# Sink attention feeding a sticky mixture of experts on one core: moving the split of the second head group, the order of GpSimd's group work, and the PSUM banks of the routing

## The chip, the core and the metric

The kernel runs on one core of one Trainium2 chip. The core has a matrix engine (PE, with its weight loads shown apart as PEld), a vector engine (DVE), a scalar engine (ACT), GpSimd (POOL) and a sync engine (SP) that issues most of the DMAs. Each engine works through its own list of instructions in order and waits on semaphores of the others. The metric is the device time of one execution in microseconds (us), lower is better; "before" and "after" are medians of several runs. An execution taken by the profiler gives the trace, with a span (first to last instruction of the program) a little shorter than its device time.

## The reference

For 4 batches, 8 heads, 768 positions and a head width of 64 the program computes attention in which a query sees the first 4 positions (sinks) and the last 128 (the window), and feeds its output to a mixture of 8 experts in which a token may stay with the expert of the token before it:

```python
keep = is_sink | in_window
scores = np.where(keep, scale * np.matmul(q, k.transpose(0, 1, 3, 2)), -1000000000.0)
a = np.exp(scores - np.max(scores, axis=-1, keepdims=True))
x = np.matmul(a / (np.sum(a, axis=-1, keepdims=True) + 1e-09), v)    # then (B, S, H * D)

logits = np.einsum('bsd,de->bse', x, w_gate)
local_gate = 1.0 / (1.0 + np.exp(-np.einsum('bsd,de->bse', x, w_local).squeeze(-1)))
for b in range(B):
    prev_e = -1
    for s in range(S):
        fresh_e = int(np.argmax(logits[b, s]))
        if s == 0 or local_gate[b, s] < 0.5: e = fresh_e
        else: e = prev_e if prev_e >= 0 else fresh_e
        prev_e = e
        p = softmax(logits[b, s])
        out[b, s] = p[e] * (np.maximum(x[b, s] @ w1[e], 0.0) @ w2[e])
```

All inputs and outputs are float32. (`softmax` stands here for three lines of the reference.)

## The kernel before

**Two halves.** Up to about 239 us of the span the kernel runs the attention with the routing of tokens to experts; after that it runs the experts one after another. The change touches the first half only, in the path for a narrow window (`attention(True)`; the other path is not run on these inputs).

**Groups and blocks.** The attention is cut into 8 groups of four heads (two groups for a batch), counted from 0 here: group g is batch g // 2. A group has 6 blocks of 128 queries, so there are 48 blocks, n = 0 to 47, and block n belongs to group n // 6. Within a block the four heads are two pairs, c = 0 and c = 1. The heart of the schedule is one loop over n that works on four blocks at once: it scores block n on PE (`score`, L635), subtracts the maximum on DVE (`out`, L647) and takes the exponential on ACT (L650), transposes the weights of block n - 1 on PE (`turn`, L665) and copies them back on ACT (`turned`, L672), turns and splits the sink part of n - 1 (L655, L676, L682, L686), multiplies block n - 2 with the values (`apply`, L696 and L701), and brings block n - 3 back into row order with its gate logits (`collect` L587, `back` L591, `finish` L607 and L611). PE, DVE and ACT run in exactly the order in which the loop is written (a manual schedule). POOL and SP are ordered by the framework's scheduler, except where `tc.issue_after` or an explicit dependency says otherwise.

**Splits.** The scores are products of float32 values, done as three products of a high and a low part. So the queries and keys of every group have to be split before its first block: a cast to the high part (`copy`, L135) and a subtraction for the low part (`low`, L140), for two pairs, keys (800 columns) and queries (768 columns). The result goes into `hq` (odd groups) or `w_a` (even groups). Group 0 is split piece by piece on DVE, ACT and POOL; all others were split on POOL alone, eight instructions for a group. `qk_split` makes four steps for a group, numbered 0: keys of pair 0, 1: queries of pair 0, 2: keys of pair 1, 3: queries of pair 1, and the table `HEADS` says at which unit (k = 2 i + c for block i of the running group) which steps of the next group are issued. An entry of `behind` becomes an explicit wait of the next cast on another instruction ("a port of its own"): in group 0 on the latest low part that POOL was given (`lows["gpsimd"]`), in later groups on DVE's L647 of the running block. Each group has a further small split on POOL, the sink rows of its values (`sinks`, L579 and L580).

**Loads.** SP issues, in an order chained by `queue`, the raw queries and keys (four buffers, so the load of a pair waits until the split of the pair four earlier has read its buffer), the values and the sink rows.

**Routing.** When the second group of a batch is done, a generator (`routing`) works through the batch's tokens in small steps that the tables `SCORED` (after the scores of a block) and `CLOSED` (at the end of a block) interleave with the blocks: gate logits and their maximum on DVE (L276 to L294), two transposes with a scan (L310, L314, L319), one-hot rows (L329, L331), positions (L358, L361), normalisation and slot numbers on DVE (L335 to L371), and six indirect DMAs that POOL issues to scatter the rows by expert (L376). For batch 0 these steps fall in blocks 14 to 23, for batch 1 in 26 to 35, for batch 2 in 38 to 45 by a table of its own; the last batch is handled after block 47. `early_rows` follows for batch 2: a count of the first expert's rows (L413, L414, L416 to L422), two loads of such rows by SP, three small DVE operations (L434 to L436), a broadcast over PE (`shown`, L439, L440) and two DVE operations on its result (L443).

**PSUM.** The transposes of the weights use a pool `ps_t` of two banks in turn; the sink turn and `back` share one bank in `ps_b`. The routing's results used that same single bank.

```python
ps_t = pool("ps_t", 2 if fast else 1, space=PS)
ps_b = pool("ps_b", 1, space=PS)
if fast:
    ps_m, m_tag = ps_b, "b"
```

Of the kernel before, what the change touches and what calls it, by code (L numbers as in the profile page):

```python
# [47 lines left out]
FILL = 5  # L48
FIRST_P = 4
SCORED = {5: 1, 6: 1, 9: 1, 10: 1}, {41: 1, 42: 1, 43: 1, 44: 1, 45: 1, 47: 1}  # L50
CLOSED = {2: 1, 3: 1, 4: 1, 5: 1, 6: 1, 9: 1, 10: 1, 11: 1}, {38: 1, 39: 2, 41: 1, 42: 1, 43: 1, 44: 2, 45: 2, 46: 1, 47: 1}
LOADS = {0: (2,), 2: (3,), 3: (0,), 4: (1,), 6: (4,), 8: (5,)}
HEADS = {4: (0, 1), 5: (2, 3)}, {2: (0, 1), 3: (2, 3)}, {0: (0, 1), 1: (2, 3)}
FIRST = 0, 2, 4, 6, 1, 3, 5, 7
NPR = HG // 2
SENG = ("vector", "gpsimd", "act", "vector"), ("act", "gpsimd", "act", "vector")
LENG = SENG[0], ("act", "gpsimd", "act", "gpsimd")
REST = (("vector", "gpsimd", "act", "gpsimd"),) * NPR
ENGS = (("gpsimd", "gpsimd", "gpsimd", "gpsimd"),) * NPR
RAW = 7200  # L60
RAW_W = RAW + 56
NZ = 4
# [12 lines left out]
def kernel(ctx, tc, qkd, vn, vs, w1, w2, nw, c_misc, c_ident, c_idw, c_small,  # L75
# [61 lines left out]
    lows, behind, opened = {}, [], []  # L137
# [402 lines left out]
    def attention(fast):  # L540
# [3 lines left out]
        with ExitStack() as st:  # L544
            def pool(nm, bufs, **kw):
                return st.enter_context(tc.tile_pool(name=nm + sfx, bufs=bufs, **kw))
# [3 lines left out]
            ps_t = pool("ps_t", 2 if fast else 1, space=PS)  # L550
            ps_a = pool("ps_a", 1, space=PS)
            ps_b = pool("ps_b", 1, space=PS)
            ps_s = pool("ps_s", 2, space=PS)
            if fast:
                ps_m, m_tag = ps_b, "b"
                pe_p = pool("pep", 2)
            else:
                ps_m, m_tag = pool("ps_m", 1, space=PS), "m"
                p1 = pool("p1", 1)
                relg = p1.tile([P, 2, S], F32, name="relg")  # L560
                nc.sync.dma_start(relg, c_all)
# [210 lines left out]
            if fast:  # L772
                ng = len(groups)
                preps = [{"heads": []} for _ in groups]
                preps[0]["heads"] = heads0
                gst = [group_steps(b, g, preps[gi]) for gi, (b, g) in enumerate(groups)]

                def head(gi, h):
                    if h == 0:
                        preps[gi]["steps"], preps[gi]["heads"] = qk_split(gi, ENGS)  # L780
                    preps[gi]["steps"][h]()

                def slot(u, gi, k):
                    nx = gi + 1
                    if gi == 0:
                        for x in LOADS.get(k, ()):
                            qk_load(x) if x > 1 else gst[nx]["load"][x]()
                        if k == RK:
                            gst[0]["sinks"]()
                    if nx >= ng:  # L790
                        return
                    for h in HEADS[gi and 2 - gi % 2].get(k, ()):
                        if gi and not h:
                            behind.append(u["dve"])
                        elif not gi:
                            behind.append(lows["gpsimd"])
                        with tc.issue_after(opened[-1].ins) if gi % 2 and h else ExitStack():
                            head(nx, h)
                        if nx == ng - 1 and h >= 1:
                            free.append(True)  # L800
                    if gi and k in (4, 5):
                        gst[nx]["load"][k - 4]()
                    if k == 2 * NBLK - 1:
                        gst[nx]["sinks"]()
                    if gi:
                        last.clear()

# [36 lines left out]
                for n in range(nb):  # L844
# [49 lines left out]
                    weights(n, now[0] if now else None)  # L894
                    steps(CLOSED, n)
                while pend:
# [3 lines left out]
                b, g = B - 1, G - 1  # L900
# [127 lines left out]
    with branch.Else():  # L1028
        attention(False)
# [299 lines left out]
    for c in range(2):  # L1329
        h, l = [t[:, c, :] for t in w1_of(1)]  # L1330
# [158 lines left out]
```

## Time and profile before

| | |
|---|---|
| median of 3 runs | 569.78 us (569.46 to 572.39) |
| profiled execution | 566.28 us, span 564.5 us |
| mean granted TensorE clock | 0.969 |
| PE busy | 525.7 us (93%) |
| DVE busy | 332.6 us (59%) |
| ACT busy | 282.8 us (50%) |
| POOL busy | 230.6 us (41%) |
| DMA | 80.55 MB, mean 143 GB/s |

Rows of the trace read: start and duration in us, engine (PE, PEld, DVE, ACT, POOL, SP; a "q" behind it is its sequencer), line of the kernel, operation, tile written <- tiles read with shapes, and the number of like instructions merged into the row. A bracket at the end gives how long the engine was idle before the row and what ended that. Rows that sum up a stretch of time give, for each engine, its busy time and in brackets its instructions, then the granted clock (1.00 is full speed) and the DMAs' share. Rows that group instructions by their form end with the total busy time, the mean of one in ns, and the idle time before them.

### The profile page before, as it was taken

To read this page: it belongs to the slowest core of one execution; us is meant where nothing else is said; L and a number is where in the kernel's file an instruction comes from. 1 tells how busy PE (TensorE), PEld (TensorE's weight loads), DVE (VectorE), ACT (ScalarE), POOL (GpSimd) and SP (SyncE) were. 2 spreads that over 40 slices of the span, in tenths; PEclk is the share of its full clock that TensorE was granted. 3 is DMA by queue.
4 is the path that set the end of the run, shared out by engine and by line. 5 is a ranking of instruction groups with operands and counts; after the bars stand their busy time and mean duration, and the time that the engine had idled before them with its cause. 6 is when DMAs were issued, how large, how long until landed. Compare 5 with 4: busy or idle time off the path is not lost. (4 is left out here: it accounts for less than half of the span.)

```text
span 564.5 us, 11848 instructions
## 1 busy us (share of the span) xinstructions
PE 525.7 (93%) x3935; PEld 449.0 (80%) x3935; DVE 332.6 (59%) x1260; ACT 282.8 (50%) x861; POOL 230.6 (41%) x196
## 2 busy tenths in 40 slices
PE   6979999889989988999999999999999899999994
PEld 3768878677877867878888888979878598889893
DVE  5647887777768867744348193735456737353321
ACT  4848888577847867253344271706324344124120
POOL 3658706760874073237350262535304434104101
PEclk8779999999979998999999999999999989999998
DMA  8354332550435035167491383848215484111000
GB/s 292 142 212 151 134 100 72 193 177 36 153 138 206 2 114 188 58 208 233 116 352 35 124 274 121 311 109 304 99 50 199 168 272 148 56 44 37 20 24 36
DMA packets 31020, 80.55 MB, mean 143 GB/s; under 512 B 3678, under 2 KB 6366, under 8 KB 30816
## 3 DMA queue, kind: packets, MB, share of 16 engines
q1 hardware_dynamic: 26064, 65.41, 34.2%
q0 software_dynamic: 4176, 12.64, 6.0%
q14 instruction: 149, 1.22, 0.7%
q8 instruction: 55, 0.90, 0.6%
q10 hardware_dynamic: 576, 0.39, 0.2%
HBM read 63.41 MB, written 16.06 MB: 141 GB/s over the span
## 5 line engine op out<-in xcount | busy, mean ns | idle before, releaser
L650 ACT ACTIVATE pef<-smf,biasf 128x264 f32<-128x264 f32 (+2 forms) x192 | 93.6, 489 | 41.5 <-DVE biasf L647 41.4
L1175 ACT ACTIVATE hq<-h 128x32 fp32r<-128x32 f32 (+4 forms) x112 | 32.1, 317 | 142.1 <-PE h L1164 92.0
L647 DVE CUSTOM_DVE_ANT_0 smf<-sf,mask 128x264 f32<-128x264 f32 (+2 forms) x192 | 66.7, 403 | 17.5 <-PE sf L635 6.4
L1140 DVE SCALAR_TENSOR_TENSOR hq<-h,hq 128x32 fp32r<-128x32 f32 (+4 forms) x112 | 34.4, 332 | 66.4 <-ACT hq L1175 66.0
L1213 PE MATMUL late<-w_a,hq 128*128 128x512 f32 (+2 forms) x288 | 69.0, 394 | 0.0
L1213 PEld LDWEIGHTS late<-w_a,hq 128*128 128x128 f32 (+2 forms) x288 | 50.8, 179 | 13.0 <-issue 0.2
L1195 POOL DMA_INDIRECT out_dram<-ot_d,oi_d x18 | 19.4, 1077 | 94.2 <-DVE ot_d L1194 74.7
L665 PE MATMUL tpf<-ident,pef 128*128 128x128 f32 x352 | 54.9, 297 | 1.9 <-ACT ptf L672 1.1
L701 PE MATMUL avf<-ptf,v 128*64 128x128 f32 x704 | 52.4, 288 | 2.7 <-issue 2.7
L672 ACT COPY ptf<-tpf 128x512 f32<-128x512 f32 (+1 forms) x96 | 51.1, 532 | 6.9 <-remote 3.4
L665 PEld LDWEIGHTS tpf<-ident,pef 128*128 128x128 f32 x352 | 40.6, 149 | 9.9 <-ACT ptf L672 3.6
L701 PEld LDWEIGHTS avf<-ptf,v 128*64 128x64 f32 x704 | 39.6, 141 | 8.3 <-issue 3.4
L1213 PE MATMUL late<-w_b,hq 128*128 128x512 f32 (+1 forms) x168 | 39.9, 393 | 0.0
L607 DVE TENSOR_TENSOR xb<-bkf,rsf 128x256 f32<-128x256 f32 x48 | 20.3, 423 | 27.7 <-ACT ptsf L682 24.9
L650 ACT ACTIVATION_READ_ACCUMULATOR pef<-smf,biasf 128x1 f32 x192 | 36.4, 189 | 0.0
L591 PE MATMUL bkf<-idw,xtf 128*128 128x146 f32 x192 | 34.5, 305 | 1.9 <-DVE xtf L587 1.5
L1213 PEld LDWEIGHTS late<-w_b,hq 128*128 128x128 f32 (+1 forms) x168 | 30.6, 184 | 7.0
L1164 PEld LDWEIGHTS h<-x_a,w_c 128*128 128x128 f32 x288 | 34.8, 192 | 1.4 <-issue 1.1
L1164 PE MATMUL h<-x_a,w_c 128*128 128x256 f32 x288 | 35.4, 284 | 0.4 <-DMA out_dram<-ot_d,oi_d 0.4
L1070 POOL TENSOR_TENSOR w_c<-raw,w_c 128x1024 fp32r<-128x1024 f32 x10 | 25.2, 2521 | 24.6 <-ACT w_c L1069 21.7
L376 POOL DMA_INDIRECT xs<-xb,slotf x24 | 23.4, 974 | 26.1 <-DVE xb L371 18.2
L1070 POOL TENSOR_TENSOR w_a<-raw,w_a 128x1024 fp32r<-128x1024 f32 x10 | 24.6, 2460 | 22.8 <-ACT w_a L1069 18.0
(228 smaller groups left out, 1081.4 us busy)
## 6 DMA issues: line engine op xcount, KB each, us to landing
raw<-in_dram SPq DMA_DIRECT2D x53, 512.0 KB
raw<-in_dram SPq DMA_DIRECT2D x14, 800.0 KB
v<-in_dram SPq DMA_DIRECT2D x7, 768.0 KB
xr_0n<-xs SPq DMA_DIRECT2D x18, 258.0 KB
raw_w<-in_dram SPq DMA_DIRECT2D x7, 512.0 KB
raw<-in_dram SPq DMA_DIRECT2D x10, 256.0 KB
xs<-zrow SPq DMA_DIRECT2D x9, 258.0 KB
xr_0r<-xs SPq DMA_DIRECT2D x8, 258.0 KB
```

Source lines behind the costliest of these rows:

```text
L376: s_i = nc.gpsimd.indirect_dma_start(out=xs[:, :], out_offset=bass.IndirectOffsetOnAxis(ap=slot[:, j:j + 1].bitcast(U32), axis=0), in_=xb[ ...
L591: mm = nc.tensor.matmul(bk[:, pr * WX:(pr + 1) * WX], blk["xt"][:, pr, :], idw[:, g * NPR + pr, :], start=True, stop=True, skip_group_chec ...
L647: u["dve"] = nc.vector.tensor_tensor_reduce(out=sm[:, :w], in0=sps[:, t, :w], in1=mk, scale=-0.125, scalar=BIG, op0=ALU.add, op1=ALU.min, ...
L650: nc.scalar.activation(pe[:, h, :w], sm[:, :w], AF.Exp, bias=bias[:, t:t + 1], scale=-1.0, accum_out=z[:, h, 0:1])
L665: nc.tensor.transpose(tp[:, t, k, :], pe[:, 2 * c + t, o:o + P], ident)
L672: nc.scalar.copy(pt[:, :, 0:nt, :], tp[:, :, 0:nt, :])
L701: nc.tensor.matmul(avt[ROWS[t], pr, :], prep["v"][:, j, 2 * pr + t, :], x["pt"][:, t, k, :], start=i < 2 and pr == 0 and k == 0, stop=pr = ...
L1070: todo += [lambda s=s: lo(out=l[:, s], in0=raw[:, s], in1=h.bitcast(F32)[:, s], op=ALU.subtract) for s in ([slice(0, FF)] if eng[1] == "po ...
L1140: nc.vector.scalar_tensor_tensor(out=d[:, :, 1, :], in0=h, scalar=0.0, in1=d.bitcast(F32)[:, :, 0, :], op0=ALU.max, op1=ALU.subtract)
L1164: nc.tensor.matmul(hs, w[:, k, fs], x, start=t == 0, stop=t == len(mm) - 1)
L1175: relu = nc.scalar.activation(d[:, :, 0, :], h, AF.Relu)
L1213: nc.tensor.matmul(o, a, w, start=t == 0, stop=t == len(mm) - 1, skip_group_check=half)
```

## The change: where the splits, the sink rows and the routing's banks go

There are six edits.

1. For group 1 alone (the second group, split during group 0) the cast of the queries moves from POOL to ACT; their low part stays on POOL (`ENGS` becomes two tables).
2. The steps of that split get other places (`HEADS[0]`): keys of pair 0 and of pair 1 after block 2, queries of pair 0 after block 3, queries of pair 1 after block 4. The explicit wait on the latest POOL low part goes with each step, so it now stands on ACT's casts too.
3. The sink rows of group 1 are issued behind the latest low part on POOL (`tc.issue_after`).
4. The steps after the first of a group's split are issued behind its first cast in all later groups; before, only in those split during an odd group.
5. The routing takes its PSUM tiles from the two banks of the transposes.
6. The table for the end of the attention has no routing step at the end of block 45 (two before) and three at the end of block 46 (one before). The steps moved are the loads of early rows and L434 to L436.

```diff
-CLOSED = {2: 1, 3: 1, 4: 1, 5: 1, 6: 1, 9: 1, 10: 1, 11: 1}, {38: 1, 39: 2, 41: 1, 42: 1, 43: 1, 44: 2, 45: 2, 46: 1, 47: 1}
+CLOSED = {2: 1, 3: 1, 4: 1, 5: 1, 6: 1, 9: 1, 10: 1, 11: 1}, {38: 1, 39: 2, 41: 1, 42: 1, 43: 1, 44: 2, 46: 3, 47: 1}
 LOADS = {0: (2,), 2: (3,), 3: (0,), 4: (1,), 6: (4,), 8: (5,)}
-HEADS = {4: (0, 1), 5: (2, 3)}, {2: (0, 1), 3: (2, 3)}, {0: (0, 1), 1: (2, 3)}
+HEADS = {4: (0,), 5: (2,), 6: (1,), 8: (3,)}, {2: (0, 1), 3: (2, 3)}, {0: (0, 1), 1: (2, 3)}
...
-ENGS = (("gpsimd", "gpsimd", "gpsimd", "gpsimd"),) * NPR
+ENGS = (("gpsimd", "gpsimd", "act", "gpsimd"),) * NPR, (("gpsimd", "gpsimd", "gpsimd", "gpsimd"),) * NPR
...
             if fast:
-                ps_m, m_tag = ps_b, "b"
+                ps_m, m_tag = ps_t, "t"
...
                     if h == 0:
-                        preps[gi]["steps"], preps[gi]["heads"] = qk_split(gi, ENGS)
+                        preps[gi]["steps"], preps[gi]["heads"] = qk_split(gi, ENGS[gi > 1])
...
-                        with tc.issue_after(opened[-1].ins) if gi % 2 and h else ExitStack():
+                        with tc.issue_after(opened[-1].ins) if gi and h else ExitStack():
                             head(nx, h)
...
                     if k == 2 * NBLK - 1:
-                        gst[nx]["sinks"]()
+                        with ExitStack() if gi else tc.issue_after(lows["gpsimd"].ins):
+                            gst[nx]["sinks"]()
```

In the rows that follow, the bracket names the queues whose semaphores an instruction waits for (DMAHW: a load; Pool, DVE, PE, Activation: that engine).

POOL's list in group 0, from the last low parts of group 0 (`w_a`) over the split of group 1 (`hq`) to the sink rows of group 1 (`srf_1`). Before:

```order
L140 TENSOR_TENSOR w_a<-raw,w_a 128x272 [waits DMAHW6_49,Activation_49]
L579 CAST srf_1_572<-sxf_1_350 96x256 [waits DMAHW2_49]
L580 TENSOR_TENSOR srf_1_572<-sxf_1_350,srf_1_572 32x256 [waits Pool_49]
L140 TENSOR_TENSOR w_a<-raw,w_a 128x272 [waits DVE_49,Pool_49]
L140 TENSOR_TENSOR w_a<-raw,w_a 128x272 [waits DMAHW3_49,DVE_49]
L140 TENSOR_TENSOR w_a<-raw,w_a 128x240 [waits Activation_49] x2
L135 CAST hq<-raw 128x800 [waits DMAHW6_49,Pool_49]
L140 TENSOR_TENSOR hq<-raw,hq 128x800 [waits Pool_49]
L135 CAST hq<-raw 128x768 [waits Pool_49]
L140 TENSOR_TENSOR hq<-raw,hq 128x768 [waits Pool_49]
L135 CAST hq<-raw 128x800 [waits DMAHW7_49,Pool_49]
L140 TENSOR_TENSOR hq<-raw,hq 128x800 [waits Pool_49]
```

and in the changed kernel, from the last low parts of group 0 on:

```order
L140 TENSOR_TENSOR w_a<-raw,w_a 128x240 [waits Activation_49] x2
L135 CAST hq<-raw 128x800 [waits DMAHW6_49,Pool_49]
L140 TENSOR_TENSOR hq<-raw,hq 128x800 [waits Pool_49]
L135 CAST hq<-raw 128x800 [waits DMAHW7_49,Pool_49]
L140 TENSOR_TENSOR hq<-raw,hq 128x800 [waits Pool_49]
L488 COPY xb_144<-small 128x6
L489 MEMSET xb_144 128x6x2
L261 CAST identb<-ident 128x128
L262 CAST identb<-small 128x128
L140 TENSOR_TENSOR hq<-raw,hq 128x768 [waits Activation_49] x2
L579 CAST srf_1_572<-sxf_1_350 96x256 [waits DMAHW2_49]
L580 TENSOR_TENSOR srf_1_572<-sxf_1_350,srf_1_572 32x256 [waits Pool_49]
```

The sink rows stood ahead of group 0's last low parts and now stand behind the whole split; the two casts of the queries are gone from POOL, and the low parts of the queries wait for ACT and stand last.

ACT's list in the changed kernel, from the end of block 3 (copy of its second transposes) to the start of block 5:

```order
L672 COPY ptf_0_2_1_418<-tpf_0_2_1_399 128x512 [waits Activation_49]
L135 CAST hq<-raw 128x768 [waits DMAHW6_49,Pool_49]
L650 ACTIVATE pef_0_4_0_439,sum_z<-smf_0_4_0_0_460,biasf_0_4_0_440 128x264 [waits DVE_49,Activation_49]
L650 ACTIVATE pef_0_4_0_439,sum_z<-smf_0_4_0_1_463,biasf_0_4_0_440 128x264 [waits DVE_49]
L672 COPY ptf_0_3_0_480<-tpf_0_3_0_466 128x512 [waits PE_49]
L682 CAST ptsf_482<-bkf_476 96x128 [waits PE_49]
L650 ACTIVATE pef_0_4_0_439,sum_z<-smf_0_4_1_0_484,biasf_0_4_1_448 128x264 [waits DVE_49]
L650 ACTIVATE pef_0_4_0_439,sum_z<-smf_0_4_1_1_487,biasf_0_4_1_448 128x264 [waits DVE_49]
L672 COPY ptf_0_3_1_490<-tpf_0_3_1_471 128x512 [waits Activation_49]
L135 CAST hq<-raw 128x768 [waits DMAHW7_49,Pool_49]
```

Before, the two `L135` rows are not there. Each waits for a load (DMAHW) and for POOL: by the explicit wait, the first for the low part of the keys of pair 1, the second for the low part of the queries of pair 0.

POOL's list around the first scatter (`L376`, end of group 3), with the split of group 5 (`hq`) and its sink rows (`srf_1`):

```order
-L135 CAST hq<-raw 128x768 x2
-L135 CAST hq<-raw 128x800
 L376 DMA xs<-xb_144,slotf_0_1812 25600x516 x6
 L135 CAST hq<-raw 128x800
-L140 TENSOR_TENSOR hq<-raw,hq 128x768
+L135 CAST hq<-raw 128x768
+L135 CAST hq<-raw 128x800
+L135 CAST hq<-raw 128x768
 L579 CAST srf_1_2323<-sxf_1_2093 96x256
-L140 TENSOR_TENSOR hq<-raw,hq 128x768
-L140 TENSOR_TENSOR hq<-raw,hq 128x800
 L488 COPY xb_144<-small 128x6
```

Three of the four casts stood ahead of the scatter and now stand behind it, and all four low parts stand behind the sink rows' cast, where one stood ahead of it. The same holds at the second scatter. The orders of PE and DVE are unchanged but for L434 to L436, which stand one block later. On SP the load of group 2's sink rows moves behind four loads of raw queries and keys, and the loads of the raw pairs 4 to 7 are chained 4, 6, 5, 7 instead of 6, 7, 4, 5.

## The prediction

> **What bounds the kernel now.** I read the page's part 1, then PE's idle time block by block in the timeline, because PE is busy for nearly the whole span.
>
> ```profile
> PE 525.7 (93%) x3935; PEld 449.0 (80%) x3935; DVE 332.6 (59%) x1260; ACT 282.8 (50%) x861; POOL 230.6 (41%) x196
> ```
>
> PE sets the end, and the change can win or lose only where PE stands still or its clock is halved during the attention. Three such places are touched. Other engines matter where PE waits for them. The first is the start of group 1 (block 6, from 31.08):
>
> ```profile
> 21.31 2.81 POOL L140 TENSOR_TENSOR w_a<-raw,w_a 128x272 fp32r<-128x272 f32 x4
> ...
> 24.19 0.85 POOL L135 CAST hq<-raw 128x800 fp32r<-128x800 f32 x1
> ...
> 27.08 0.82 POOL L135 CAST hq<-raw 128x768 fp32r<-128x768 f32 x1
> ...
> 33.63 0.44 PE L635 MATMUL sf<-hq 64*128 64x128 f32 x4 [2.00 <-POOL hq L135]
> ...
> 35.51 0.47 PE L635 MATMUL sf<-hq 64*128 64x128 f32 x2 [1.44 <-POOL hq L140]
> ...
> 41.17 0.97 PE L635 MATMUL sf<-hq 64*128 64x256 f32 x12
> ```
>
> PE waits 3.44 us for POOL's split and block 7 starts at 41.17, 10.1 us after block 6. The windows of 3.41 us in which the clock changes (PE, PEld, DVE, ACT, POOL busy; clock):
>
> ```profile
> 30.82:34.23 3.41, 1.24 (x16) 0.79 (x12) 2.02 (x10) 2.31 (x9) 3.27 (x3) 1.00 0.66 238
> 34.23:37.65 3.42, 2.14 (x10) 2.03 (x11) 0.58 (x5) 0.59 (x1) 1.87 (x5) 0.50 0.30 65
> 37.65:41.06 3.41, 3.41 (x25) 3.11 (x23) 0.99 (x4) 1.51 (x6) 0.00 (x0) 0.50 1.01 412
> ...
> 102.49:105.90 3.41, 1.79 (x21) 1.45 (x19) 3.28 (x11) 0.41 (x1) 2.44 (x4) 1.00 0.48 192
> 105.90:109.32 3.42, 3.34 (x39) 2.83 (x39) 2.63 (x14) 2.71 (x11) 2.81 (x3) 1.00 0.35 134
> ...
> 157.09:160.51 3.42, 1.76 (x18) 1.53 (x20) 3.34 (x15) 1.08 (x5) 2.54 (x4) 1.00 0.09 35
> 160.51:163.92 3.41, 3.41 (x28) 2.96 (x25) 1.62 (x6) 2.13 (x8) 2.50 (x4) 0.50 0.55 206
> ```
>
> The stall is paid twice: a window with 1.24 us of PE work is followed by half clock. So is one with 1.76; one with 1.79 is not.
>
> The second place is block 23, and likewise block 35, at the scatter:
>
> ```profile
> 102.86 2.39 POOL L135 CAST hq<-raw 128x768 fp32r<-128x768 f32 x3 [1.69 <-issue]
> ...
> 103.06 0.69 DVE L338 TENSOR_TENSOR exf<-exf,smf 128x48 f32<-128x48 f32 x1
> ...
> 103.67 0.84 DVE L367 TENSOR_TENSOR slf<-rksf,ohs 128x48 f32<-128x48 f32 x1
> ...
> 104.44 0.87 DVE L368 TENSOR_TENSOR exf<-exf,ohs 128x48 f32<-128x48 f32 x1
> ...
> 105.85 1.15 POOL L376 DMA_INDIRECT xs<-xb,slotf  x1 [0.59 <-DVE pkf L655]
> ...
> 105.86 0.28 PE L676 MATMUL bkf<-ident,pkf 128*96 128x128 f32 x1 [1.62 <-DVE pkf L655]
> ...
> 114.53 0.29 DVE L647 CUSTOM_DVE_ANT_0 smf<-sf,mask 128x128 f32<-128x128 f32 x1 [2.40 <-remote]
> ...
> 158.67 0.29 PE L676 MATMUL bkf<-ident,pkf 128*96 128x128 f32 x1 [1.62 <-DVE pkf L655]
> ...
> 167.33 0.29 DVE L647 CUSTOM_DVE_ANT_0 smf<-sf,mask 128x128 f32<-128x128 f32 x1 [2.42 <-PE bkf L591]
> ...
> 201.38 0.21 DVE L338 TENSOR_TENSOR exf<-exf,smf 128x48 f32<-128x48 f32 x1
> ```
>
> With a POOL cast running, L338 takes 0.69 instead of the 0.21 it takes in block 45, and each of the three ends with one of POOL's casts. PE waits 1.62 for what is queued behind them on DVE. The later long wait of DVE ends 8.68 us after the first scatter starts, with clock 1.00, and 8.7 after it in block 36, with clock 0.50; so I tie it to the scatter and expect it to stay.
>
> The third is the bank of the routing:
>
> ```profile
> 79.36 1.09 PE L665 MATMUL tpf<-ident,pef 128*128 128x128 f32 x8
> ...
> 79.47 0.79 ACT L314 COPY kff<-tff 8x768 bf16<-8x768 bf16 x1 [0.19 <-PE tff L310]
> ...
> 88.70 0.77 PE L591 MATMUL bkf<-idw,xtf 128*128 128x146 f32 x4 [0.74 <-DVE xtf L587]
> ...
> 214.25 0.35 PE L439 MATMUL shown<-early_f,one_row 1*128 1x1 f32 x2 [2.49 <-ACT pef L650]
> ...
> 215.84 0.21 DVE L443 TENSOR_SCALAR hide<-shown_f 128x1 int32<-128x1 f32 x2 [1.52 <-ACT shown_f L440]
> ```
>
> **Edits 1 to 3, group 1.** Costs by form:
>
> ```profile
> L140 POOL TENSOR_TENSOR hq<-raw,hq 128x768 fp32r<-128x768 f32 x8 | 14.5, 1824 | 0.2
> ...
> L135 POOL CAST hq<-raw 128x768 fp32r<-128x768 f32 x8 | 6.4, 825 | 3.8 <-issue 3.4 <-PE sf L635 0.3
> ...
> L531 ACT CAST w_a<-raw 128x512 fp32r<-128x512 f32 x8 | 4.6, 626 | 0.0
> ...
> L135 ACT CAST w_a<-raw 128x256 fp32r<-128x256 f32 x3 | 1.1, 403 | 2.3 <-DMA raw<-in_dram 2.3
> ...
> 20.04 0.39 POOL L579 CAST srf<-sxf 96x256 fp32r<-96x256 f32 x1 [4.27 <-DMA sxf<-in_dram]
> ...
> 19.67 0.69 ACT L135 CAST w_a<-raw 128x240 fp32r<-128x240 f32 x2
> ...
> 25.10 0.52 ACT L650 ACTIVATE pef<-smf,biasf 128x264 f32<-128x264 f32 x1 [0.71 <-DVE biasf L647]
> ```
>
> POOL loses two casts (2 x 0.83) and, from the front of its list, the sink rows with a wait of 4.27 for their load. Its last low parts of group 0 then wait only for ACT's casts (19.67 to 20.36), so POOL reaches the split of group 1 at about 21.4, 2.8 earlier. Two key casts with their low parts (27.08 - 24.19 = 2.89 each) end at 27.2. But ACT's cast of the first queries waits for exactly that, by the explicit wait that came with the step, and ACT is in order: its block 4, which began at 25.10, is queued behind it. A cast of 768 columns is not in the trace: from 626 ns at 512 and 403 at 256 columns it is 0.85 us, at least 0.63. So ACT resumes at 27.2 + 0.8 = 28.0, 2.9 late. The low part of those queries then follows on POOL until 29.8, while ACT's second cast comes only after block 4 at about 31.2: no second wait. Its low part ends at 33.9.
>
> The stall thus moves: PE finds the weights of block 4 late in block 5. It has 0.9 us of work in 27.41 to 28.3, half the transposes from 29.6, the rest from 31.25 when ACT has emptied the bank. Block 6 begins at 33.7 instead of 31.08, but its data is there. At full clock block 7 begins at 37.9. The window 27.41 to 30.82 holds 0.9 + 0.66 = 1.6 us, below the 1.76 that was followed by half clock. One halved window (30.82 to 34.23) puts block 6 at 35.4 and block 7 at 39.3; two put block 7 at 41.0. Against 41.17 the gain is 3.3, 1.9 or 0.2. I take 1.9, the case nearest to the rows: the half clock ended after a window that was full.
>
> The rule of the Trainium skill's TensorE: Matmul & The Clock Gate (What's actually happening) speaks for a better result: half rate follows a window of about 3.4 us that is idle. By it the new stall would cost no clock, and the gain here would be 3.3. The rows of this trace differ, with half clock after windows half busy.
>
> **Edit 4, blocks 23 and 35.** The three casts leave the stretch before the scatter; POOL has nothing else there. The DVE chain falls from 0.69 + 0.84 + 0.87 to about 3 x 0.21, so PE's wait of 1.62 goes, 1.6 at each place, 3.2 in sum (no less than 1.3 each, if the sinks' low part just ahead of it lasts longer). The scatter starts 1.6 earlier and keeps its own cost. What is late next is POOL's work behind it:
>
> ```profile
> 113.33 0.86 POOL L135 CAST hq<-raw 128x800 fp32r<-128x800 f32 x1
> ...
> 117.94 0.39 POOL L579 CAST srf<-sxf 96x256 fp32r<-96x256 f32 x1 [1.97 <-PE avf L696]
> ...
> 124.09 0.73 POOL L580 TENSOR_TENSOR srf<-sxf,srf 32x256 fp32r<-32x256 f32 x1
> ...
> 126.79 0.21 DVE L282 TENSOR_TENSOR eqf<-lgf,mxf 128x48 f32<-128x48 f32 x1
> ```
>
> In the old clock: casts until 116.6, the sinks' cast still at 117.94 (it waits for PE), 0.3 of small work, four low parts 118.7 to 126.1, the sinks' low part until 126.9. That touches the routing's L282 at 126.79. Cost 0.2 at each of blocks 28 and 40, 0.4 in sum; 0 if POOL is 0.2 faster, 1.4 if a whole 0.73 is waited out twice. Group 3's split (during group 2) ends at about 73, ahead of the same step of batch 0. The splits themselves are due a group later: nothing.
>
> **Edit 5, the banks.** In the blocks with L314 the second half of the transposes now takes the bank that the routing has just filled, and must wait until ACT has copied it: 79.47 + 0.79 = 80.26 against a start at 79.9, about 0.45. Two such blocks for each of three batches. The block that follows them holds a PE wait for DVE (0.74 at 88.70), which swallows most of it: I keep 0.25 for a batch, 0.75 in sum, between 0 and 3 x 0.9. The other routing copies are done before their bank is due. In block 46 `shown` no longer waits for the shared bank and starts about 1.1 earlier, but L443 on DVE waits for ACT's L440, which stays behind two casts: gain 0.15, at most 1.2 (PE's own lead). **Edit 6** and SP's order: three DVE operations of 0.13 moved by a block, loads ahead of need: 0.
>
> **Sum.** 1.9 + 3.2 - 0.4 - 0.75 + 0.15 = 4.1. The expert half is PE-bound behind it and moves forward as a whole. From the profiled 566.28 (span 564.5) that is 562.2; the median of the runs is 3.5 above the profiled execution, so 569.78 - 4.1 = **565.7**.
>
> **Rivals.** (a) *The stall only changes its engine*: two halved windows, group 1 gains 0.2, total 2.4, 567.4. For it: in the stall quoted above half clock lasted two windows. (b) *The clock holds* in group 1 (3.3) and the bank waits are swallowed: 3.3 + 3.2 - 0.4 + 0.15, 6.2, 563.5; the clock page's rule would give this, the 1.76 row speaks against it. (c) *Slower: the port moves with the casts.* POOL's four low parts now all stand behind the sinks' cast, which waits for PE. If they end three low parts (5.5 us) later than worked out, L282 and its followers each wait out one of 1.82: two in block 28, three in block 40, 9.2 in all, less 4.5 gained elsewhere: 4.7 slower, 574.5. It decides from about 3 us of delay (5 us lost). Against it: POOL has no other wait behind the sinks' cast. The Trainium skill's SBUF — State Buffer (SBUF: two separate sides) says that a DVE operation with two SBUF inputs is shut out for the whole of a POOL operation that started first; L338 above agrees, and by it (c) is the price of any overrun. (d) *The change doesn't do what it says* in block 23: the DVE chain stays slow, because the scatter's own preparation or the sinks' low part slows it; gain 0.9, 568.9.
>
> **Numbers.** Forecast 0.43, (a) 0.25, (b) 0.15, (c) 0.10, (d) 0.07. Half a per cent (2.85 us) is about what a measurement can tell from no change. Faster by that: 0.38 of the forecast's 0.43, all of (b), 0.04 of (a), 0.57. Slower: (c), 0.10, and 0.01 of the rest. Same: 0.32. The range goes from the best ends together (3.3 + 3.2 + 1.2 = 7.7 less than the fastest run before, 569.46: 561.7) to the worst ends of edits 4 and 5 with (a) (0.2 + 3.2 - 1.4 - 2.7 = -0.7: 570.5), so that little more than (c) is left out; the forecast's own range is 563.5 to 567.5.
>
> **What would show it.** Right: ACT idle for over 2 us ahead of its first L135 in group 1, no PE wait on POOL in block 6, block 7 between 38 and 41; L338 to L368 at 0.2 each in blocks 23 and 35 with no wait at L676; a PE wait of about 0.45 between the transposes of blocks 17 and 18. Wrong: long L282 or L283 in blocks 28 or 40 (c), a DVE wait of 2.4 missing after the scatter, or half clock elsewhere.

## The result: 3.2 us faster by the medians, the forecast 4.1

| | before | after |
|---|---|---|
| median of 20 runs each | 569.66 us (566.72 to 573.05) | 566.49 us (562.83 to 571.90) |
| profiled execution | 566.28 us, span 564.5 | 563.35 us, span 561.6 |

The ratio is 0.9946 with a 95% interval of 0.9921 to 0.9971, that is 1.7 to 4.5 us faster. Part 1 of the page of the changed kernel:

```profile
PE 526.0 (94%) x3935; PEld 445.6 (79%) x3935; DVE 331.2 (59%) x1260; ACT 284.2 (51%) x863; POOL 227.4 (40%) x194
```

ACT has the two casts more that POOL has less, and everything else kept its work: the change moved waits (and, as it turns out, windows of half clock). Both profiled executions lie about 3.3 below their medians, so their difference of 2.9 can be split up by place. The table measures from the first L635 of one block to that of another, on both traces, beside the prediction's terms.

| stretch of blocks | before | after | won | predicted |
|---|---|---|---|---|
| 0 to 6, start of group 1 | 34.61 | 32.24 | 2.4 | 1.9 |
| 17 to 19 and 29 to 34, banks | 38.35 | 38.87 | -0.5 | -0.5 |
| 40 to 44, banks of the third batch, and POOL's low parts at block 40 | 22.17 | 22.38 | -0.2 | -0.45 |
| 23 to 25, first scatter | 16.60 | 16.64 | 0.0 | 1.6 |
| 35 to 37, second scatter | 16.60 | 15.98 | 0.6 | 1.6 |
| 28, POOL behind the scatter | 4.61 | 4.60 | 0.0 | -0.2 |
| 45 and 46, third scatter and `shown` | 14.09 | 13.07 | 1.0 | 0.15 |

The terms of group 1 and of the banks came out. The largest one, the two scatters, did not. The timeline of the changed kernel at the start of group 1 (start, duration, engine; the bracket is the idle time before it and its releaser):

```profile
27.31 0.83 ACT L135 CAST hq<-raw 128x768 fp32r<-128x768 f32 x1 [2.83 <-POOL hq L140]
...
28.05 0.51 ACT L650 ACTIVATE pef<-smf,biasf 128x264 f32<-128x264 f32 x1
...
29.67 0.65 PE L665 MATMUL tpf<-ident,pef 128*128 128x128 f32 x4 [1.27 <-ACT ptf L672]
...
31.15 0.84 ACT L135 CAST hq<-raw 128x768 fp32r<-128x768 f32 x1
...
31.31 1.12 PE L665 MATMUL tpf<-ident,pef 128*128 128x128 f32 x4 [0.98 <-ACT ptf L672]
...
32.07 1.82 POOL L140 TENSOR_TENSOR hq<-raw,hq 128x768 fp32r<-128x768 f32 x1 [2.04 <-ACT hq L135]
```

ACT stands still 2.83 us for POOL's low part of the keys and starts block 4's exponentials at 28.05; PE pays in block 5 with two waits, of 1.27 and 0.98. Block 6, whose 3.44 us of waits are gone, starts at 35.16 and block 7 at 38.81.

At the first scatter, block 23 with the wait gone, and then what follows it:

```profile
101.00 0.21 DVE L338 TENSOR_TENSOR exf<-exf,smf 128x48 f32<-128x48 f32 x1
...
101.13 0.20 DVE L367 TENSOR_TENSOR slf<-rksf,ohs 128x48 f32<-128x48 f32 x1
101.25 0.20 DVE L368 TENSOR_TENSOR exf<-exf,ohs 128x48 f32<-128x48 f32 x1
...
102.03 0.27 PE L676 MATMUL bkf<-ident,pkf 128*96 128x128 f32 x1
...
102.62 1.13 POOL L376 DMA_INDIRECT xs<-xb,slotf  x1 [3.50 <-DVE xtf L587]
...
109.07 0.27 PE L701 MATMUL avf<-ptf,v 128*64 128x128 f32 x1 [0.35 <-issue]
...
109.80 0.31 PE L701 MATMUL avf<-ptf,v 128*64 128x128 f32 x1 [0.46 <-issue]
...
111.20 0.38 PE L701 MATMUL avf<-ptf,v 128*64 128x128 f32 x2 [1.09 <-issue]
...
111.23 0.29 DVE L647 CUSTOM_DVE_ANT_0 smf<-sf,mask 128x128 f32<-128x128 f32 x1 [3.07 <-remote]
```

L338, L367 and L368 take 0.2 each and PE no longer waits at L676: block 23 lasts 4.08 instead of 5.90. Then PE gets its multiplications out one at a time while it waits for nothing that the profile shows ("issue"), and DVE's long wait ("remote": the profile finds no releaser on this core) ends 8.61 us after the scatter began, as it did before (8.68). That is the prediction's "keeps its own cost". But the scatter starts 2.45 us into block 23, where it started 3.63 us into it before: 1.2 earlier and not 1.6, so the end of DVE's wait lies 0.57 later in block 24 (6.98 into it, 6.41 before), and block 24 grows by 0.52. The other thing that the prediction did not have is the clock. The windows of 3.41 us at the start of group 1, around the first scatter and around the second (PE, PEld, DVE, ACT, POOL busy; granted clock; DMA):

```profile
27.63:31.04 3.41, 1.42 (x16) 0.97 (x14) 1.17 (x5) 3.41 (x12) 2.11 (x3) 1.00 0.02 4
31.04:34.45 3.41, 3.14 (x17) 3.01 (x19) 2.44 (x13) 3.31 (x11) 2.30 (x3) 0.50 0.97 355
34.45:37.87 3.42, 3.42 (x43) 3.11 (x41) 2.12 (x14) 2.43 (x9) 0.58 (x1) 1.00 0.81 286
109.55:112.96 3.41, 1.96 (x17) 1.37 (x17) 1.41 (x9) 1.67 (x7) 3.37 (x5) 1.00 0.37 144
112.96:116.37 3.41, 3.03 (x18) 2.91 (x20) 2.65 (x14) 2.68 (x11) 1.41 (x5) 0.50 0.00 0
160.75:164.16 3.41, 1.95 (x19) 1.36 (x17) 0.51 (x4) 0.88 (x4) 3.06 (x4) 1.00 0.60 230
164.16:167.57 3.41, 3.32 (x20) 2.77 (x21) 2.88 (x15) 2.44 (x9) 2.07 (x3) 0.50 0.02 7
```

A window of half clock, a halved window for short, costs at most 1.7 (half of 3.41). There is one in group 1, as taken in the forecast, and one behind each of the two scatters. In the trace of before the first scatter was followed by none:

```profile
112.73:116.15 3.42, 2.03 (x18) 1.30 (x17) 1.33 (x8) 1.73 (x9) 3.23 (x3) 1.00 0.37 145
116.15:119.56 3.41, 2.97 (x37) 2.59 (x36) 3.05 (x16) 2.68 (x11) 1.62 (x2) 1.00 0.01 2
```

So block 25, in which the halved window begins, grows by 1.34. That and the 0.52 of block 24 are what block 23 had won. At the second scatter the trace of before already had two halved windows, from 160.5 on, behind the wait in block 35; after, there is one, and 0.6 is won.

### The profile page after: what moved, and what is told of

Same layout as the page of the kernel before. It is cut to its first block, busy times and chain, and to the rows that moved or that the text cites. A ratio compares the mean times of both kernels' runs of the same rounds, so it can differ in the third digit from the quotient of the medians.

```text
span 561.6 us, 11850 instructions
## 1 busy us (share of the span) xinstructions
PE 526.0 (94%) x3935; PEld 445.6 (79%) x3935; DVE 331.2 (59%) x1260; ACT 284.2 (51%) x863; POOL 227.4 (40%) x194
## 5 line engine op out<-in xcount | busy, mean ns | idle before, releaser
L650 ACT ACTIVATE pef<-smf,biasf 128x264 f32<-128x264 f32 (+2 forms) x192 | 93.5, 489 | 37.0 <-DVE biasf L647 34.8
L647 DVE CUSTOM_DVE_ANT_0 smf<-sf,mask 128x264 f32<-128x264 f32 (+2 forms) x192 | 66.6, 403 | 13.1 <-PE bkf L591 3.8
L665 PE MATMUL tpf<-ident,pef 128*128 128x128 f32 x352 | 56.6, 296 | 7.0 <-ACT ptf L672 3.3
L665 PEld LDWEIGHTS tpf<-ident,pef 128*128 128x128 f32 x352 | 39.4, 147 | 17.9 <-ACT ptf L672 6.8
L672 ACT COPY ptf<-tpf 128x512 f32<-128x512 f32 (+1 forms) x96 | 51.0, 531 | 4.2 <-remote 2.4
L650 ACT ACTIVATION_READ_ACCUMULATOR pef<-smf,biasf 128x1 f32 x192 | 36.3, 189 | 0.0
L376 POOL DMA_INDIRECT xs<-xb,slotf x24 | 23.5, 979 | 30.8 <-DVE xb L371 17.3
```

What stands on the lines that cost most here:

```text
L376: s_i = nc.gpsimd.indirect_dma_start(out=xs[:, :], out_offset=bass.IndirectOffsetOnAxis(ap=slot[:, j:j + 1].bitcast(U32), axis=0), in_=xb[ ...
L647: u["dve"] = nc.vector.tensor_tensor_reduce(out=sm[:, :w], in0=sps[:, t, :w], in1=mk, scale=-0.125, scalar=BIG, op0=ALU.add, op1=ALU.min, ...
L650: nc.scalar.activation(pe[:, h, :w], sm[:, :w], AF.Exp, bias=bias[:, t:t + 1], scale=-1.0, accum_out=z[:, h, 0:1])
L665: nc.tensor.transpose(tp[:, t, k, :], pe[:, 2 * c + t, o:o + P], ident)
L672: nc.scalar.copy(pt[:, :, 0:nt, :], tp[:, :, 0:nt, :])
```

## The experiments

Theory at the outset: the start of group 1, the banks and the wait in block 23 are as predicted, and the scatter takes back what block 23 wins. The rivals are in each run's expectation. The runs were made in four series, each on one chip with the kernel before beside them. On three of these chips the kernel before took 558 to 560 us, on one 569.41, as in the first comparison; ratios are always to the kernel before on the same chip.

**Edits 1 to 3 alone.** The diff is that of the change for `HEADS`, `ENGS`, `qk_split` and the sink rows; the rest is as before.

> The kernel before with edits 1 to 3 alone (group 1's queries cast on ACT, the new places of the steps, sink rows behind). Theory A (the stall moves to block 5 and is paid there once): block 7 starts near 38.8 as in the changed kernel against 41.17, so 2.4 us faster than before. Rival B (most of the measured gain is from the other edits): below 1 us.

Ratio 0.9963 (0.9924 to 1.0003): the times alone can't tell it from no change. Block 7 starts at 38.87, as in the changed kernel, but block 0 began 0.57 earlier in this trace than in that of before. From the first L635 on, blocks 0 to 6 take 32.87, against 34.61 in the first trace of before and 34.49 in the run with edit 4 alone on this chip. So the stall moved to block 5 (8.56, with one halved window) as theory A has it, and 1.6 to 1.7 was won in this execution, not 2.4.

**Edit 4 alone.**

```diff
-                        with tc.issue_after(opened[-1].ins) if gi % 2 and h else ExitStack():
+                        with tc.issue_after(opened[-1].ins) if gi and h else ExitStack():
```

> The kernel before with edit 4 alone (the casts of groups 4 and 6 behind the scatters). As predicted, PE's wait of 1.62 at L676 goes in blocks 23 and 35 and is won: 3.2 us faster. Theory A (the scatter takes it back: blocks 24 and 25 grow by what block 23 loses, part of it as a window of half clock): blocks 23 to 25 together 16.6 as before, 35 to 37 within 0.7 of before, 0 to 0.7 us faster.

Ratio 1.0001 (0.9971 to 1.0032): nothing won, give or take 1.7 us, but not for the reason of theory A. On this chip blocks 23 to 25 took 11.44, against 13.25 in the run with edits 1 to 3, where they stand as before; 35 to 37 likewise. So 1.8 was won at each scatter, and nothing followed the scatter. More than that was lost in blocks 28 (7.36 against 4.59) and 40 and 41 (12.58 against 9.71). The timeline there, POOL's and DVE's rows of the run with edit 4 alone, and the windows at block 28:

```profile
104.57 1.13 POOL L376 DMA_INDIRECT xs<-xb,slotf  x1 [3.51 <-DVE xtf L587]
...
115.81 7.31 POOL L140 TENSOR_TENSOR hq<-raw,hq 128x800 fp32r<-128x800 f32 x4
...
121.51 1.68 DVE L282 TENSOR_TENSOR eqf<-lgf,mxf 128x48 f32<-128x48 f32 x1
123.19 0.72 POOL L580 TENSOR_TENSOR srf<-sxf,srf 32x256 fp32r<-32x256 f32 x1
123.22 0.76 DVE L283 TENSOR_TENSOR eqf<-eqf,small 128x48 f32<-128x48 f32 x1
...
124.52 0.28 PE L676 MATMUL bkf<-ident,pkf 128*96 128x128 f32 x1 [2.01 <-DVE pkf L655]
...
171.95 1.36 DVE L282 TENSOR_TENSOR eqf<-lgf,mxf 128x48 f32<-128x48 f32 x1
173.31 0.72 POOL L580 TENSOR_TENSOR srf<-sxf,srf 32x256 fp32r<-32x256 f32 x1
173.34 0.76 DVE L283 TENSOR_TENSOR eqf<-eqf,small 128x48 f32<-128x48 f32 x1
...
122.53:125.94 3.41, 1.34 (x11) 1.11 (x13) 3.35 (x13) 0.67 (x3) 1.30 (x2) 1.00 0.67 240
125.94:129.35 3.41, 3.41 (x31) 2.84 (x30) 2.58 (x14) 2.78 (x10) 0.00 (x0) 0.50 0.24 93
```

121.51 lies in block 28, 171.95 in block 40. L282 begins under the last of POOL's four low parts and ends with it (123.12 and 123.19), and L283 is shut out by the low part of the sink rows: 1.68 and 0.76 instead of 0.2 each. PE then waits 2.01 for what stands behind them on DVE, and a halved window follows, at block 40 likewise (from 177.13). This is the prediction's rival (c), mechanism and place; its half clock the prediction had not priced. The same rows of the changed kernel on the first chip:

```profile
115.93 7.32 POOL L140 TENSOR_TENSOR hq<-raw,hq 128x800 fp32r<-128x800 f32 x4
123.33 0.73 POOL L580 TENSOR_TENSOR srf<-sxf,srf 32x256 fp32r<-32x256 f32 x1
...
124.79 0.21 DVE L282 TENSOR_TENSOR eqf<-lgf,mxf 128x48 f32<-128x48 f32 x1
```

There POOL is through 0.7 us before L282. From the first scatter to L282 it is 22.2 us on that chip and 16.9 in the run with edit 4 alone, and to the end of POOL's work 21.4 and 19.3: so on the chip of the first comparison the stretch behind the scatter is longer by 5.3 us for DVE, and by 2.1 for POOL.

**The scatter on two chips.** DVE's rows of block 24 in the run with edit 4 alone, whose first scatter began at 104.57:

```profile
107.76 0.42 DVE L587 COPY xtf<-avf 128x256 f32<-128x256 f32 x1
108.10 0.28 DVE L647 CUSTOM_DVE_ANT_0 smf<-sf,mask 128x128 f32<-128x128 f32 x1
...
108.73 0.28 DVE L647 CUSTOM_DVE_ANT_0 smf<-sf,mask 128x128 f32<-128x128 f32 x1
```

Here no wait stands between the four L647 of block 24, where the chip above had one of 3.07. Yet the scatter is the same: the first and the last of its six DMA issues start 6.54 us apart (6.55 there), its packets lie between 1.7 and 9.0 us after the first issue (1.7 and 9.1), with a median of 168 ns for a packet of 4,128 bytes in both. Call it the hold: on the chips near 569 DVE's L647 ends a wait of 2.4 to 3.7 us, 7.9 to 8.7 us after each of the first two scatters began, in all six traces; on the three chips near 559 it does so in none of the eight.

**Without ACT's wait.** On the changed kernel:

```diff
-                        elif not gi:
+                        elif not gi and not h % 2:
                             behind.append(lows["gpsimd"])
-                        with tc.issue_after(opened[-1].ins) if gi and h else ExitStack():
+                        with tc.issue_after(opened[-1].ins if gi else lows["keys"].ins) if h and (gi or h == 3) else ExitStack():
                             head(nx, h)
+                        if not gi and h == 2:
+                            lows["keys"] = lows["gpsimd"]
```

> The changed kernel without the explicit wait of ACT's query casts on POOL's low parts, and with POOL's order keys 0, queries 0, keys 1, queries 1. Theory A (that wait alone makes the stall in block 5): ACT's wait of 2.83 ahead of its cast goes, block 5 takes 3.8 instead of 7.75, block 6 starts at 31.2 instead of 35.16, no half clock there: 3.5 to 4 us faster than the changed kernel, 6.5 to 7 faster than before. Rival B (POOL is the bound, so group 1's data is late anyway): the wait comes back in block 6 for POOL's low parts, gain below 1 us.

Ratio 0.9917 (0.9876 to 0.9957), 4.6 faster than before. ACT and PE of this run:

```profile
23.81 0.83 ACT L135 CAST hq<-raw 128x768 fp32r<-128x768 f32 x1
24.62 0.52 ACT L650 ACTIVATE pef<-smf,biasf 128x264 f32<-128x264 f32 x1
...
30.30 0.77 PE L635 MATMUL sf<-hq 64*128 64x128 f32 x10
31.81 0.33 PE L635 MATMUL sf<-hq 64*128 64x128 f32 x2 [0.74 <-POOL hq L140]
```

The cast starts at 23.81, block 5 takes 3.75, and blocks 0 to 6 take 28.95, against 32.87 in the run with edits 1 to 3 on the same chip: 3.9 won, theory A at its place. (The edit also lets the first queries' low part run ahead of the second keys' on POOL; the two were not tried apart.) POOL's last low part still comes 0.74 late. The whole is 2 us short of the expectation since edit 4 costs here again more than it wins: block 28 takes 6.61, blocks 40 and 41 14.24.

**The scatters in two halves.** On the changed kernel, for the first two batches (shortened; with `paced` a tile of one column, `pace` the list of DVE's L647, a step of the routing more at the end of the next block, and L488 and L489 two blocks later):

```diff
+            if sfx == "f" and b < 2 and j in AT:
+                yield
+                mark = nc.gpsimd.memset(paced, 0.0)
+                tc.add_manual_dep(mark.ins, pace[-1].ins.name, mybir.DependencyInfo(
+                    mybir.DependencyClass.Sync, mybir.DependencyReason.DATA), reason="a block later")
+            with tc.issue_after(mark.ins) if sfx == "f" and b < 2 and j >= AT[0] else ExitStack():
-            s_i = nc.gpsimd.indirect_dma_start(
+                s_i = nc.gpsimd.indirect_dma_start(
...
+    AT = 3,
```

> The changed kernel with each of the first two scatters cut in two halves of three DMAs, the second half behind DVE's L647 of the next block and behind POOL's casts (the row numbers of the next batch are written two blocks later). Theory A (six scatters in a row hold back PE's signals for 8.6 us; three hold them for 4.3, which the work in flight covers): blocks 23 to 25 take 12 to 13.5 instead of 16.6, 3 to 8 us faster in sum than the changed kernel. Rival B (every scatter DMA has its own price, or the price is at the end of the DMAs): the stall comes twice, no gain or a loss of 1 to 3 us.

Ratio 0.9988 (0.9957 to 1.0020). It fell on a chip without the hold, so the question was not put: blocks 24 and 25 take 4.16 and 3.18, as with one scatter. But ACT's wait is still in this kernel, and POOL's low parts end later: blocks 28 and 40 with 41 take 8.22 and 14.67 (with some half clock), worse than any other run.

**The change once more, and edit 6 alone,** on a chip with the hold. Edit 6 is the line `CLOSED` of the change.

> The changed kernel unaltered, on the chip of this series. Theory A (edit 4 trades the wait in blocks 23 and 35 for DVE shut out by POOL's low parts in blocks 28 and 40, where the scatter does not hold PE back): group 1 won 2.4, blocks 23 and 35 won 1.8 each, blocks 28 and 40 with 41 lost 2 to 3.3 each, the banks lost 0.25 for a batch, block 46 won 1 to 1.4: 0 to 2.5 us faster than before. Where the scatter holds PE back as in the first traces: 3 us faster. Rival B (the changed kernel gains the same wherever the scatter is quick): over 6 us faster.

Ratio 0.9941 (0.9909 to 0.9972), again 3 us. Blocks 23 to 25 take 16.89, 28 takes 4.61, 35 to 37 15.89: as in the first trace.

> The kernel before with edit 6 alone (the loads of early rows and L434 to L436 one block later). As predicted: nothing, block 46 within 0.2 us of before. Rival: the gain of about 1 us in block 46 comes from here, not from the bank.

One execution, 574.65 beside a median of 569.41, so it has no gain to show. Blocks 45 and 46 take 14.27 (14.09 before), which says little alone, since half clock sets in within block 46 here. But PE's L439 still waits for ACT's exponentials (L650, 0.81 here, 2.49 before), and in every run with the bank of the change that wait is gone. So the gain there needs the bank; the bank without edit 6 was not run. Since edit 6 doesn't touch the scatters, this trace shows them a second time as they were: blocks 23 to 25 take 18.25 and 35 to 37 17.36, against 16.60 for both in the first, and block 26 takes 4.15 against 3.04. Where PE is held, one kernel's executions differ by a halved window or two.

**Edit 4 undone, no wait of ACT, the routing in the single bank** (the early count stays in the transposes' banks). Beside the diff of the run without ACT's wait:

```diff
-                            pend.append(routing(b, *r, sfx, ps_m, m_tag))
+                            pend.append(routing(b, *r, sfx, *((ps_b, "b") if fast else (ps_m, m_tag))))
-                        with tc.issue_after(opened[-1].ins) if gi and h else ExitStack():
+                        with tc.issue_after(opened[-1].ins if gi % 2 else lows["keys"].ins) if h and (gi % 2 or not gi and h == 3) else ExitStack():
```

> The changed kernel without ACT's explicit wait, with edit 4 undone and with the routing in the single bank again (the early count alone in the transposes' banks). Theory A: group 1 won 6.2, block 46 won 1 to 1.4, banks nothing, blocks 23, 28, 35, 40 as before: 7 to 7.6 us faster than before, and 2.5 to 3.5 faster than the run without ACT's wait alone. Rival B (the banks, not edit 4, made blocks 28 and 40 long): blocks 28 and 40 long again or no faster than that run.

> The kernel with edit 4 undone once more, beside the one above on the same chip. Where the scatter holds nothing back, theory A: blocks 23 and 35 at 5.9 and blocks 28 and 40 at 4.6 and 5.2, so 7 to 8 us faster than before and 2 to 3 slower than the one above. Rival (edit 4 pays even so): more than 4 slower. Where it holds PE back: 5 to 8 us faster, no difference from the one above.

With the hold 0.9874 (0.9829 to 0.9919), without it 0.9891 (0.9847 to 0.9935). Blocks 17 to 19 take 13.37 again, as before the change. Without the hold block 46 keeps its gain (4.77, against 6.14 and 5.86 in the runs without the bank); with it, it takes 8.78, half of it at half clock. So the bank costs 0.25 for a batch, and only the early count has something from it. Blocks 28 and 40 take 4.59 and 5.24 without the hold. They were long with edit 4 alone, where the bank was the old one, so it was edit 4 and not the bank that made them long. In exchange the wait in blocks 23 and 35 is back, and in both profiled executions half clock sets in within block 23 as well. The windows of the second one, on a chip without the hold:

```profile
95.67:99.09 3.42, 2.00 (x22) 1.62 (x20) 3.29 (x11) 0.66 (x3) 2.39 (x3) 1.00 0.55 216
99.09:102.50 3.41, 3.13 (x25) 2.57 (x25) 2.61 (x14) 2.46 (x9) 2.61 (x3) 0.71 0.28 107
102.50:105.91 3.41, 3.41 (x22) 3.28 (x23) 1.97 (x13) 2.22 (x8) 2.50 (x4) 0.50 0.56 207
```

Blocks 23 to 25 take 15.87 there, against 13.25 with the same wait and the full clock. That is a miss of the expectation, which had 5.9 for blocks 23 and 35: they take 6.77 and 7.48, and the run is 4.0 slower than the next one on the same chip, not 2 to 3.

**Edit 4 kept, and two of its four casts on ACT.** Beside the bank's line above and the lines for the wait (those of the run without ACT's wait):

```diff
-HEADS = {4: (0,), 5: (2,), 6: (1,), 8: (3,)}, {2: (0, 1), 3: (2, 3)}, {0: (0, 1), 1: (2, 3)}
+HEADS = {4: (0,), 5: (2,), 6: (1,), 8: (3,)}, {2: (0, 1), 3: (2, 3)}, {0: (0, 2), 1: (1,), 3: (3,)}
-                        preps[gi]["steps"], preps[gi]["heads"] = qk_split(gi, ENGS[gi > 1])
+                        preps[gi]["steps"], preps[gi]["heads"] = qk_split(gi, ENGS[gi % 2 == 0])
```

> The changed kernel without ACT's wait, edit 4 kept, the routing in the single bank, and the query casts of groups 3, 5 and 7 on ACT, at the end of the first two blocks of the group before. Theory A (POOL is late by 2.6 us at L282; two casts of 0.83 less and the same low parts end 1.7 earlier): L282 takes below 1 us in blocks 28 and 40, blocks 23 and 35 4.1, blocks 24 and 25 at most 0.7 longer for ACT's casts: 8 to 10.5 us faster than before. Rival B (ACT has no room): blocks 25 and 26 grow by 1 us or more, not faster than with edit 4 undone.

> The kernel with ACT's query casts for groups 3, 5 and 7 once more, to see it on a chip on which the scatter holds nothing back, if this series falls on one. Theory A (POOL's low parts shut DVE out in blocks 28 and 40, and end 1.7 earlier here): L282 below 1 us, block 28 below 5.2 against 6.6 to 7.4 with POOL's casts, block 40 below 5.8 against 7.2 to 8.6; 9 to 11 us faster than before. Rival B (ACT becomes the bound): blocks 25 and 26 grow by over 1 us together, and no more than 7 us faster. On a chip where the scatter holds PE back: 6 to 8 us faster, as the first time.

With the hold 0.9873 (0.9818 to 0.9927); without it 0.9821 (0.9763 to 0.9879), 10 us faster than before. With the hold that is 7.2 us, not the 8 to 10.5 expected, and no more than with edit 4 undone (0.9874), the outcome that rival B had. Blocks 25 and 26 take 5.93 and 3.77 there, against 5.55 and 3.05 in the changed kernel on that chip, under two halved windows; without the hold they take 3.19 and 3.03, so ACT's casts alone do not lengthen them. DVE and POOL at block 28 of the run without the hold:

```profile
114.31 1.89 POOL L140 TENSOR_TENSOR hq<-raw,hq 128x800 fp32r<-128x800 f32 x1
...
116.28 0.72 POOL L580 TENSOR_TENSOR srf<-sxf,srf 32x256 fp32r<-32x256 f32 x1
116.41 0.66 DVE L282 TENSOR_TENSOR eqf<-lgf,mxf 128x48 f32<-128x48 f32 x1
117.10 0.21 DVE L283 TENSOR_TENSOR eqf<-eqf,small 128x48 f32<-128x48 f32 x1
...
117.85 0.28 PE L676 MATMUL bkf<-ident,pkf 128*96 128x128 f32 x1 [0.44 <-DVE pkf L655]
```

The low parts are through before L282 and only the sink rows' low part still touches it: 0.66, and a wait of 0.44 at PE in place of 2.01. Blocks 23 to 25 keep 11.43, block 28 takes 4.94, blocks 40 and 41 9.75: theory A, on such a chip. ACT's casts show nowhere in blocks 24 to 26. Block 27 is 0.37 longer, since the second of them (109.10 to 109.95) takes the 0.66 us in which ACT stood still there with edit 4 undone: ACT is late with its copies, and PE's second half of the transposes starts at 112.95, behind ACT's L672, 0.8 after the first instead of at once. Blocks 15 and 39 are longer by 0.3 to 0.4 too.

**The same with the scatters in halves,** two casts of POOL between them, twice.

> The kernel with ACT's query casts, and the first two scatters in two halves of three DMAs with two casts of POOL between them. Where the scatter holds PE back, theory A (the hold is six scatters long): PE's gaps at L701 in blocks 24 and 36 go, blocks 23 to 26 take below 16 against 16.6 to 20.8, 3 to 8 us faster than with one scatter. Rival B (each scatter DMA has its price): no gain, gaps in blocks 24 and 25. Where nothing is held back: POOL ends 0.3 later, L282 up to 1 us, same time within 1 us.

> The kernel with ACT's query casts and the first two scatters in halves once more, in the hope of a chip on which the scatter holds PE back (before near 569). There, theory A (the hold grows with the number of scatter DMAs in a row): PE's gaps at L701 in blocks 24 and 36 go or halve, DVE's wait ends 4 to 5 us after the first scatter instead of 8.6, blocks 23 to 26 take below 17.5 against 20.8 with one scatter of six, 2 to 5 us faster than that kernel's 0.9873. Rival B (each scatter DMA has its own price, wherever it stands): the gaps stay, now in blocks 24 and 25, and the ratio is 0.985 to 0.99. On a chip without the hold: 0.978 to 0.986 as before, and blocks 24 and 25 at 4.16 and 3.19.

0.9818 (0.9771 to 0.9866) and 0.9816 (0.9783 to 0.9849), no different from the kernel with whole scatters. Both fell on chips without the hold, so whether halves shorten it stays untried.

## Why the prediction was right, and where it was not

**Group 1** (predicted 1.9, measured 2.4 in the pair of traces). Step by step: ACT idle 2.9 (2.83), resuming at 28.0 (28.05), the second cast at 31.2 (31.15) with no second wait, one halved window, block 6 at 35.4 (35.16), block 7 at 39.3 (38.81). Four traces have these edits with ACT's wait: blocks 0 to 6 take 31.43 to 32.88, 32.36 on average, against 34.61 in three traces without the edits, so 2.3 on average. In the seven traces without ACT's wait they take 28.60 to 28.95, 3.6 less again: the stall was ACT's place behind POOL. That edits 1 to 3 move the stall rather than remove it, was right.

**Banks** (predicted -0.75, measured -0.73). PE waits in blocks 17 and 18 for ACT's copy:

```profile
77.16 0.79 ACT L314 COPY kff<-tff 8x768 bf16<-8x768 bf16 x1 [0.19 <-PE tff L310]
...
78.00 0.66 PE L665 MATMUL tpf<-ident,pef 128*128 128x128 f32 x4 [0.29 <-ACT kff L314]
```

The blocks are longer by 0.46 and 0.45, and block 19, where PE had waited for DVE, is shorter by 0.65. Where the routing goes back to the single bank, all of that goes.

**`shown`** (predicted 0.15, measured 1.0):

```profile
211.04 0.38 PE L439 MATMUL shown<-early_f,one_row 1*128 1x1 f32 x2 [1.35 <-ACT ptf L672]
211.35 1.20 PE L635 MATMUL sf<-hq 64*128 64x264 f32 x12
...
213.76 0.21 DVE L443 TENSOR_SCALAR hide<-shown_f 128x1 int32<-128x1 f32 x2 [1.38 <-ACT shown_f L440]
```

The step that failed is "L443 on DVE waits for ACT's L440, which stays behind two casts". The observation was right: L443 comes 9.96 us after the start of block 46, and 9.91 before. The conclusion was not. PE waits for nothing behind L443; its wait ahead of `shown` is 1.35 instead of 2.49, and the 1.1 is PE's to keep. The value, 1.0 here and 0.8 to 1.4 in block 46 on the chips without the hold, lies about the bound of 1.2.

**Edit 4** (predicted 3.2 less 0.4, measured 0.6 in the pair of traces). The wait of 1.62 went and block 23 shrank by 1.82. The steps that failed are "1.6 at each place", counted as a gain of the whole, and "The scatter starts 1.6 earlier and keeps its own cost". The scatter starts 1.2 earlier, and its stall is followed by halved windows in some executions and not in others; the sum had taken the trace of before, with none in block 25, for the rule. "Half clock elsewhere" was one of the prediction's own signs of being wrong, and it was there. With the two traces of each kernel on such chips (blocks 23 to 26: 19.64 and 22.41 before, 19.68 and 19.93 after; blocks 35 to 37: 16.60 and 17.36, 15.98 and 15.89) the gain is 1.2 and 1.0 on average, and two traces of each kernel can't fix it.

**The small cost of 0.4 behind the scatter** is the step that matters elsewhere. It set POOL's end (126.9) beside L282 (126.79) in the clock of one chip. That margin is made by the hold, which delays DVE more than POOL. Without it L282 comes 3.2 us earlier against POOL's work, and rival (c), held for 0.10, takes 2.8 in block 28 and 2.9 in blocks 40 and 41, so that edit 4 alone is worth nothing (1.0001). Its place, the instruction shut out and the size of one low part were as written; the price was 5.7 and not 9.2. What was wrong was "POOL has no other wait behind the sinks' cast" as the argument against it, since POOL need not be later for it: DVE can be earlier. The pair of traces that the forecast was about shows none of this, so there the term was 0.

**The end.** The total fell inside the forecast's own range because 0.5 more in group 1 and 0.9 more at `shown` stand against 2.2 less at the scatters. That these errors offset each other is luck; the mechanisms of group 1 and of the banks are not.

**Clock and port.** By the Trainium skill's TensorE: Matmul & The Clock Gate (What's actually happening), half rate follows an idle window. The traces differ from that: in the changed kernel windows with 1.42, 1.83, 1.95 and 1.96 us of PE work were followed by half clock, so here a window more than half full can be too. In the trace of before windows with 1.79 and 2.03 were followed by full clock, so PE's busy time alone doesn't give the border that the prediction saw between 1.76 and 1.79.

The Trainium skill's SBUF — State Buffer (SBUF: two separate sides) has it that a DVE operation with two SBUF inputs is shut out for as long as a GpSimd operation that reads SBUF and started first runs. L282's 1.68 and L283's 0.76 above agree.

## What to carry to other kernels

A cast that is moved to an idle engine brings its waits with it: ask of each explicit wait whether the new engine still needs it (here it cost 3.6 of 5.9 us), and of each shared bank which of its users had waited. A margin between two engines that share a port is only as good as the delay that makes it; work it out also for the case that the delay goes away, which here was another chip. When work that shuts out DVE must go behind something, make it shorter as well: two of four casts on ACT turned a loss of 2.8 in block 28 into 0.35. The kernel with that, without ACT's wait and with the routing in its old bank is 1.8% faster than the kernel before on the chips without the hold. On a chip with it that is 1.3%, which the kernel with edit 4 undone reaches as well.

## What the runs showed of the hardware

The same program differs by 11 us between chips (569.41 against 558.39 for the kernel before), and most of it lies at the three scatters: blocks 23 to 25, 35 to 37, and 45 and 46 take 16.60, 16.60 and 14.09 on the chip of the first comparison, and 13.25, 13.25 and 11.63 in the run with edits 1 to 3 on the other, 9.2 in sum, and up to 11.7 with the second trace of the old scatters. Behind the first two scatters PE's multiplications are then up to 1.1 us apart with no wait that the profile shows, and DVE waits 2.4 to 3.7 us, with the DMA's issues, packets and durations alike. What on the chip holds them is not settled: no run here takes the scatters away or spaces them on a chip that has the hold, and whether the scatter is the cause, and not only the place, is not shown.
